# First token steps and first weights loaded by SyncE as fp32, token steps split between SyncE and GpSimd, casts on three engines

## The chip, the cores and the metric

One core of one Trainium2 chip runs the kernel. The metric is the device time of one execution in microseconds (us). The kernel before takes 766.0 us, the median of three runs from 765.8 to 766.04.

The engines are named as in the profile: PE is TensorE's matmuls, PEld its weight loads, DVE is VectorE, ACT is ScalarE, POOL is GpSimd, SP is SyncE.

## The reference

A causal convolution over tokens with seven taps per head (a softmax over the taps), followed by a gated feed-forward layer:

```python
w = softmax(weight)                          # (8 heads, 7 taps)
x_pad = concatenate([zeros((B, 6, D)), x])   # x: (8, 4096, 192)
out[b, s, h, g] = sum_k w[h, k] * x_pad[b, s + k, h, g]   # 24 channels a head
x = out.reshape(32768, 192)
gate = maximum(x @ w_gate, 0)                # w_gate: (192, 1536)
val = x @ w_val                              # w_val:  (192, 1536)
return (gate * val) @ w_out                  # w_out:  (1536, 192)
```

All inputs and the output are fp32. The kernel computes in fp16 with fp32 sums.

## The kernel before

**Tiling.** The eight sequences are two streams of four: stream 0 is batches 0 to 3, stream 1 batches 4 to 7, and both are worked on side by side. 192 channels are three groups (c) of 64; stream 0 sits in partitions 0 to 63, stream 1 in 64 to 127. A unit is 1024 tokens of each stream, in two windows of 512, and there are 16 units. For each window `gate_val` makes the hidden values: for each of twelve slices f of 128 hidden columns, six matmuls with Wg and six with Wv (L541), a ReLU on ScalarE (L552) and a product on VectorE (L553). `project` then multiplies with Wo (L570) and writes the result.

**The weights.** Wg and Wv are held in fp16 twice, in partitions 0 to 63 and 64 to 127, since the two streams need them on their own halves of the array. `load_w(s)` (L167) loads slice s of both, cut at columns 0, 128, 384, 640, 896, 1152 and 1536, by GpSimd with a cast to fp16 on the way, into the lower half. `both_halves` (L175) copies a slice to the upper half: on VectorE for slices 0 and 1, on GpSimd (`pool_halves`) for the others. Slice 0 serves f = 0, slice 1 serves f = 1 and 2, slice 2 serves f = 3 and 4, and so on.

**The convolution.** From the second unit on it is spread over VectorE, ScalarE and GpSimd, with tap values from `tap` (ten small transfers on SyncE, L310, copied to the upper half by GpSimd at L665) and tokens turned by transposing transfers. The first unit has no time for that, so TensorE does it with band matrices: `bands[h]` holds the taps of head h on its diagonals, and x with tokens in partitions is the other operand. A window of 512 tokens is cut in five steps (jj); step 0 has the first 96 tokens of the sequence and no rows ahead of it, steps 1 to 4 have 104 tokens each and 6 rows from before. `conv_dense(0, c, ...)` (L352) does the first window for one c, 40 matmuls in turn over steps and streams; `first_block` (L387) calls it for the three c and copies the result from PSUM to `xc` (L392). The second window (`second_block`) comes between f = 4 and f = 5 of the first.

**The loads at the start.** x of the first window goes to the tile `xts[0]` (`x_h` in the profile; fp16, indices row, step, stream, channel). Stream 0's steps 1 to 4 are loaded by SyncE as fp32 (L122) into `stage`, which is a piece of the tile `room` (`prods` in the profile) that has no other use until later; step 0 of both streams likewise (L138). ScalarE casts the former to fp16 (L317, in two pieces by channels), VectorE the latter (L335). Stream 1's steps 1 to 4 are loaded by GpSimd with the cast on the way (L127). The order is written by hand (`manual_schedule`): every engine executes its instructions in the order in which the program issues them, and an instruction that waits holds all that is behind it on its engine. At the start these orders are:

- SyncE: the taps' weights (L101), stream 0's steps 1 to 4 (L122), step 0 of both streams (L138), the ten `tap` transfers (L310).
- GpSimd: a memset (L126), stream 1's steps 1 to 4 (L127), the select for `spaced` (L128), weight slices 0, 1, 2 (each Wg then Wv), the tokens of the second window (`load_x(1)`, L86), slice 3, the copies of slice 2, slice 4, and so on.
- ScalarE: the softmax' exponentials, the casts of L317, bands of heads 4 to 7 (L329), then copies of `xc`.
- VectorE: the small chain to the band matrices (ending at L329 for heads 0 to 2), the cast of L335, the band of head 3, the copies of slice 0 of Wg and Wv, one `xc` copy, the copies of slice 1.
- TensorE: matmuls without use that keep it busy (L154), the matmuls that make the bands (L272, L292), the 120 convolution matmuls, then L541.

In `conv_dense` the first c takes steps 1 to 4 of stream 0, steps 1 to 4 of stream 1, and step 0 of both; the other c take steps 1, 2, 3, 4, 0 with both streams in each:

```python
late = (1, 2, 3, 4, 0)
both = [(jj, (0, 1)) for jj in late]
if g == 0 and c == 0:
    both = [(jj, (st,)) for st in range(2) for jj in late[0:4]] + both[4:]
```

For f = 0 of the first window the gate and value matmuls go c by c, so that the first needs only the first 64 channels of `xc`, and slice 0 of Wg and Wv in both halves.

## Time and profile before

| what | value |
|---|---|
| median of three runs | 766.0 us |
| span of the profiled execution | 764.4 us |
| TensorE busy | 760.3 us, 99% of the span |
| VectorE, ScalarE, GpSimd busy | 705.6, 600.9, 378.4 us |
| bytes moved by the transfers | 56.00 MB |
| granted TensorE clock in the page's 40 slices | 9 tenths or more in each |

Times in the timeline and in the chain are microseconds from the start of the span: first the start, then the length, then the engine, the line of the kernel, the operation, what it writes and reads, its shape and how many are merged in the line. What stands in brackets is idle time of the engine just before, and what ended it. A line that issues a transfer shows how long the issue took on its engine, not when the data lands; that is in the list of transfers, as the time from issue to landing in the last column. A line of the windows has the stretch, its length, the busy time of the engines with the number of instructions in brackets, the granted clock, the share of the transfer engines and GB/s.

### The profile page before, as it was taken

What the parts mean: (1) busy time and instruction counts of PE and PEld (TensorE: products, weight loads), DVE (VectorE), ACT (ScalarE), POOL (GpSimd) and SP (SyncE); (2) the same over time, 40 slices, a digit from 0 to 9 for tenths busy, and PEclk for the clock granted to TensorE, in tenths of its full rate; (3) what the DMA queues carried; (4) which work ended last, traced back from release to release, by engine and by line L of the source; (5) the groups of instructions that cost most, each with busy time, mean ns of one, the idle gap of its engine ahead of it and who ended that gap; (6) DMA issues with size and microseconds to landing.
All of it is one profiled execution on the core that took longest, in us unless ns stands there. A gap on an engine that the chain in (4) does not pass through costs nothing.

```text
span 764.4 us, 25103 instructions
## 1 busy us (share of the span) xinstructions
PE 760.3 (99%) x10929; PEld 501.3 (66%) x10929; DVE 705.6 (92%) x763; ACT 600.9 (79%) x735; POOL 378.4 (50%) x244
## 2 busy tenths in 40 slices
PE   9999999999999999999999999999999999999998
PEld 5494674947649476584855848567494674947648
DVE  7998999999999999999999999999999999999891
ACT  6787887878878887887878878787787887876571
POOL 9419448093571926729175390853909347090000
PEclk9999999999999999999999999999999999999999
DMA  9969039290452805528073271722819134220202
GB/s 123 134 102 148 7 96 81 65 111 22 95 67 83 97 23 107 49 85 94 30 112 40 85 94 44 120 16 90 89 44 125 13 97 60 66 48 15 71 1 84
DMA packets 131830, 56.00 MB, mean 73 GB/s; under 512 B 96392, under 2 KB 131720, under 8 KB 131720
## 3 DMA queue, kind: packets, MB, share of 16 engines
q1 hardware_dynamic: 90680, 38.81, 23.9%
q0 software_dynamic: 40896, 15.50, 20.3%
q8 instruction: 85, 1.39, 0.8%
q14 instruction: 25, 0.20, 0.1%
q10 hardware_dynamic: 144, 0.10, 0.0%
HBM read 31.48 MB, written 25.17 MB: 74 GB/s over the span
## 4 chain that ended last, share of the span: by engine, by line
PE 99%; DVE 0%; ACT 0%; issue 0%
PE ps L541 65%; PE ps L570 32%; PE ps L619 1%; PE ps L377 0%; PE ps L154 0%; PE ps L411 0%; DVE band L329 0%; PE ps L272 0%; ACT acc L596 0%; PE ps L292 0%
## 5 line engine op out<-in xcount | busy, mean ns | idle before, releaser
L553 DVE TENSOR_TENSOR hT<-gr,ps 128x1024 f16<-128x1024 f16 (+1 forms) x386 | 469.0, 1216 | 36.6 <-ACT gr L552 9.4
L552 ACT ACTIVATE gr<-ps 128x1024 f16<-128x1024 f32 (+1 forms) x386 | 392.9, 1019 | 101.9 <-PE ps L541 99.7
L491 POOL TENSOR_TENSOR prods<-prods 128x1344 f32<-128x1344 f32 x70 | 212.4, 3034 | 290.0 <-DVE prods L487 286.7
L541 PE MATMUL ps<-xc,Wg 64*128 64x512 f16 x2304 | 311.9, 376 | 0.0
L541 PE MATMUL ps<-xc,Wv 64*128 64x512 f16 x2304 | 311.9, 376 | 0.0
L570 PEld LDWEIGHTS <-hT 64*128 64x128 f16 x5952 | 245.9, 94 | 3.7
L570 PE MATMUL ps<-Wo,hT 64*128 64x192 f16 x5952 | 248.1, 243 | 0.0
L541 PEld LDWEIGHTS <-Wv 64*128 64x128 f16 x2304 | 129.8, 94 | 118.5 <-DVE hT L553 0.3
L541 PEld LDWEIGHTS <-Wg 64*128 64x128 f16 x2304 | 112.3, 94 | 132.8 <-issue 0.2
L515 DVE SCALAR_TENSOR_TENSOR acc<-x_r,tap,acc 128x576 f32<-128x576 f16 x225 | 165.3, 813 | 0.0
L485 ACT ACTIVATE prods<-x_r,tap 128x448 f32<-128x448 f16 x222 | 130.1, 660 | 0.0
L596 ACT COPY out_s<-ps 128x768 f32<-128x768 f32 (+1 forms) x64 | 45.5, 711 | 51.3 <-PE ps L570 40.0
L203 POOL DMA_DIRECT2D x_e<-in_x_dram x58 | 47.0, 823 | 16.6 <-ACT acc L501 12.8
L465 POOL COPY x_p<-x_e 128x960 f16<-128x960 f16 (+1 forms) x58 | 50.3, 906 | 1.2 <-DMA x_e<-in_x_dram 1.1
L491 POOL TENSOR_TENSOR xc<-prods 128x1344 f16<-128x1344 f32 x14 | 42.4, 3029 | 1.1
L515 DVE SCALAR_TENSOR_TENSOR xc<-x_r,tap,acc 128x576 f16<-128x576 f16 x45 | 34.1, 813 | 0.0
L501 ACT ACTIVATE acc<-x_r,tap 128x576 f32<-128x576 f16 x45 | 31.4, 763 | 0.0
L487 DVE TENSOR_SCALAR prods<-x_r,tap 128x448 f32<-128x448 f16 x70 | 26.6, 450 | 0.0
L596 DVE COPY out_s<-ps 128x384 f32<-128x384 f32 (+1 forms) x16 | 8.7, 541 | 11.9 <-PE ps L619 9.4
L619 PE MATMUL ps<-Wo,hT 128*128 128x192 f16 x96 | 8.1, 246 | 0.0
L619 PEld LDWEIGHTS <-hT 128*128 128x128 f16 x96 | 7.9, 98 | 0.2 <-issue 0.2
L154 PE MATMUL ps<-const-bfloat16-1.0 128*128 128x512 bf16 (+1 forms) x9 | 3.9, 572 | 0.8 <-PEq L719 0.8
(54 smaller groups left out, 56.3 us busy)
## 6 DMA issues: line engine op xcount, KB each, us to landing
out_dram<-out_s SPq DMA_DIRECT2D x62, 384.0 KB, 2.7
x_e<-in_x_dram POOLq DMA_DIRECT2D x34, 192.0 KB, 7.4
x_e<-in_x_dram POOLq DMA_DIRECT2D x24, 240.0 KB, 5.6
x_r<-x_p SPq DMA_TRANSPOSE x131, 5.1
Wo<-in_moe_w_out_dram POOLq DMA_DIRECT2D x1, 576.0 KB, 7.3
x_h<-in_x_dram POOLq DMA_DIRECT2D x2, 210.0 KB, 4.8
Wg<-in_moe_w_gate_dram POOLq DMA_DIRECT2D x4, 96.0 KB, 4.1
Wv<-in_moe_w_val_dram POOLq DMA_DIRECT2D x4, 96.0 KB, 4.0
```

The costliest lines, as they stand in the source:

```text
L203: first = nc.gpsimd.dma_start(out=xe[:, j0 + start : j0 + n, st, :, :].rearrange("p j c r -> p j (c r)"), in_=bass.AP(tensor=x.tensor, off ...
L465: nc.gpsimd.tensor_copy(out=xp[:, j0 : j0 + n, :, st, :], in_=xe[:, j0 : j0 + n, st, :, :])
L485: engine.activation(out=out, in_=in_, func=ACTF.Copy, scale=scale)
L487: engine.tensor_scalar(out=out, in0=in_, scalar1=scale, scalar2=None, op0=ALU.mult)
L491: nc.gpsimd.tensor_tensor(out=pr[:, 0] if k < KW - 1 else xc[v + 1][:, :, LDVE:UNIT], in0=pr[:, 0], in1=pr[:, k], op=ALU.add,)
L501: nc.scalar.activation(out=accs[v][:, c, :], in_=shifted(v, c, 0, 0), func=ACTF.Copy, scale=tap[:, c, 0:1],)
L515: nc.vector.scalar_tensor_tensor(out=xc[v][:, c, 0:LDVE] if k == KW - 1 else acc[:, c, :], in0=shifted(v, c, k, 0), scalar=tap[:, c, k : k ...
L541: nc.tensor.matmul(out=pss[i][:, st, :], lhsT=W[64 * st : 64 * st + 64, c, 128 * f : 128 * (f + 1)], rhs=xcb[64 * st : 64 * st + 64, c, WI ...
L552: nc.scalar.activation(out=gr[:, sts], in_=pss[0][:, sts], func=ACTF.Relu)
L553: nc.vector.tensor_tensor(out=h[:, f, sts], in0=gr[:, sts], in1=pss[1][:, sts], op=ALU.mult)
L570: mm = nc.tensor.matmul(out=outs[q], lhsT=h[64 * r : 64 * r + 64, f, st, 128 * q : 128 * (q + 1)], rhs=Wo[64 * r : 64 * r + 64, f, :], sta ...
L596: one(out=dst[:, step * j : step * j + step], in_=src[:, step * j : step * j + step])
```

## The change

SyncE loads steps 1 and 2 of stream 0 and, as a transfer of its own, steps 1 and 2 of stream 1, both as fp32 to `stage`. GpSimd loads steps 3 and 4 of stream 0 with the cast on the way, then makes the select, then loads steps 3 and 4 of stream 1.

After step 0 of both streams SyncE loads weight slice 0 of Wg and of Wv as fp32, to places behind `stage` in the same tile (`first_w`). GpSimd's `load_w(0)` and VectorE's copies of slice 0 go away. `cast_w` writes both halves of a slice 0 from `first_w`, two casts each: Wv's on GpSimd, after `load_w(2)` and ahead of `load_x(1)`; Wg's on VectorE, where the copies were.

ScalarE casts steps 1 and 2 of stream 0, the same of stream 1, and step 0 of both, which VectorE did before. The first window's convolution takes the steps in the order 1, 2, 0, 3, 4 with both streams in each, for all three c; the second window's order stays.

```diff
@@ -112,19 +112,20 @@
 
     xts[0] = xpool.tile([128, GSUB, 2, D], F16, name="x_h")
 
-    def body(st):
+    def body(st, jj):
         return bass.AP(
             tensor=x.tensor,
-            offset=x.offset + (NB * st * S + FIRST - PAD) * D,
-            ap=[[D, SUB], [DSUB * D, GSUB - 1], [1, D]],
-        )
-
-    nc.sync.dma_start(out=stage(0, SUB, 0, 1, 1, GSUB - 1), in_=body(0))
+            offset=x.offset + (NB * st * S + FIRST - PAD + DSUB * (jj - 1)) * D,
+            ap=[[D, SUB], [DSUB * D, 2], [1, D]],
+        )
+
+    for st in range(2):
+        nc.sync.dma_start(out=stage(0, SUB, st, 1, 1, 2), in_=body(st, 1))
     ones = const.tile([128, SUB], FP)
     nc.vector.memset(ones[:], 1.0)
     spaced = const.tile([SUB, KW, SEG + 2 * GAP], FP)
     nc.gpsimd.memset(spaced[:], 0.0)
-    nc.gpsimd.dma_start(out=xts[0][0:SUB, 1:GSUB, 1, :], in_=body(1))
+    nc.gpsimd.dma_start(out=xts[0][0:SUB, 3:GSUB, 0, :], in_=body(0, 3))
     nc.gpsimd.affine_select(
         out=spaced[:, :, GAP : GAP + SEG],
         in_=ones[0:SUB, 0 : KW * SEG].rearrange("p (k s) -> p k s", k=KW),
@@ -134,6 +135,7 @@
         base=0,
         channel_multiplier=1,
     )
+    nc.gpsimd.dma_start(out=xts[0][0:SUB, 3:GSUB, 1, :], in_=body(1, 3))
     nc.vector.memset(stage(0, 32, 0, 2, 0, 1), 0.0)
     nc.sync.dma_start(
         out=stage(PAD, FIRST, 0, 2, 0, 1),
@@ -141,6 +143,19 @@
             tensor=x.tensor, offset=x.offset, ap=[[D, FIRST], [NB * S * D, 2], [1, D]]
         ),
     )
+
+    def first_w(i):
+        at = room[0:64, 0, 0, 0:1]
+        return bass.AP(
+            tensor=at.tensor,
+            offset=at.offset + 2 * D * GSUB + NCH * 128 * i,
+            ap=[at.ap[0], [128, NCH], [1, 128]],
+        )
+
+    for i, src in enumerate((moe_w_gate, moe_w_val)):
+        nc.sync.dma_start(
+            out=first_w(i), in_=src.rearrange("(c p) f -> p c f", p=64)[:, :, 0:128]
+        )
     spare = const.tile([H, 1], FP)
     nc.scalar.activation(spare[:], ones[0:H, 0:1], ACTF.Exp)
 
@@ -218,9 +233,13 @@
                     )
                 yield
 
-    load_w(0)
+    def cast_w(copy, i):
+        for p0 in (0, 64):
+            copy(out=(Wg, Wv)[i][p0 : p0 + 64, :, 0:128], in_=first_w(i))
+
     load_w(1)
     load_w(2)
+    cast_w(nc.gpsimd.tensor_copy, 1)
     load_rest(load_x(1))
     load_w(3)
     pool_halves(2)
@@ -313,11 +332,13 @@
             )
             r += n
 
-    for cols in (slice(0, 64), slice(64, D)):
+    for st in range(2):
         nc.scalar.copy(
-            out=xts[0][0:ROWS0, 1:GSUB, 0, cols],
-            in_=stage(0, ROWS0, 0, 1, 1, GSUB - 1)[:, :, cols],
-        )
+            out=xts[0][0:ROWS0, 1:3, st, :], in_=stage(0, ROWS0, st, 1, 1, 2)
+        )
+    nc.scalar.copy(
+        out=xts[0][0 : FIRST + PAD, 0, :, :], in_=stage(0, FIRST + PAD, 0, 2, 0, 1)
+    )
     bands = {}
 
     def fill_band(a, heads, copy):
@@ -332,9 +353,6 @@
         )
 
     fill_band(0, [0, 1, 2], nc.vector.tensor_copy)
-    nc.vector.tensor_copy(
-        out=xts[0][0 : FIRST + PAD, 0, :, :], in_=stage(0, FIRST + PAD, 0, 2, 0, 1)
-    )
     fill_band(0, [3], nc.vector.tensor_copy)
     fill_band(1, [4, 5], nc.scalar.copy)
     fill_band(1, [6, 7], nc.scalar.copy)
@@ -349,26 +367,18 @@
     PLACE = {0: (0, 0, 0), 1: (0, 0, 1), 3: (0, 1, 0), 4: (0, 1, 1)}
     PLACE |= {6: (1, 0, 0), 7: (1, 0, 1), 2: (1, 1, 0), 5: (1, 1, 1)}
 
-    def conv_dense(g, c, ps, bank):
+    def conv_dense(g, c, ps, bank, steps=(1, 2, 3, 4, 0)):
 
 
         xt = xts[g]
-        if g == 0 and c == 0:
-            xc[0] = xcpool.tile([128, NCH, UNIT], F16, name="xc")
-            both_halves(nc.vector.tensor_copy, 0, Wg)
-            both_halves(nc.vector.tensor_copy, 0, Wv)
         toks = GROUPS[g][1]
         t0 = toks[0]
         ends = toks[1:] + [t0 + WIN]
-        late = (1, 2, 3, 4, 0)
-        both = [(jj, (0, 1)) for jj in late]
-        if g == 0 and c == 0:
-            both = [(jj, (st,)) for st in range(2) for jj in late[0:4]] + both[4:]
-        for jj, sts in both:
+        for jj in steps:
             col, n = toks[jj] - t0, ends[jj] - toks[jj]
             rows = n + PAD
             for second in range(2):
-                for st in sts:
+                for st in range(2):
                     for k2 in range(2):
                         k = 2 * c + k2
                         h0, h1 = 32 * k // G, (32 * k + 31) // G
@@ -385,9 +395,11 @@
                         )
 
     def first_block():
+        xc[0] = xcpool.tile([128, NCH, UNIT], F16, name="xc")
+        cast_w(nc.vector.tensor_copy, 0)
         for c in range(NCH):
             ps = psum.tile([128, 2, 512], FP, name="ps")
-            conv_dense(0, c, ps, 0)
+            conv_dense(0, c, ps, 0, (1, 2, 0, 3, 4))
             copy = nc.vector.tensor_copy if c == 1 else nc.scalar.copy
             copy(out=xc[0][:, c, 0:WIN], in_=ps[:, 0, :])
```

## Prediction

> **What bounds the kernel now.** I read the page first, then the chain of waits in order of time, then the timeline of the first 16 us, the same stretch in windows, and the transfers of the first 20 us.

> ```profile
> span 764.4 us, 25103 instructions
> PE 760.3 (99%) x10929; PEld 501.3 (66%) x10929; DVE 705.6 (92%) x763; ACT 600.9 (79%) x735; POOL 378.4 (50%) x244
> ...
> 5.09 0.52 DVE band L329
> ...
> 5.65 2.08 PE ps L377 x106
> 7.72 6.66 PE ps L541 x60
> ...
> 57.46 31.08 PE ps L541 x288
> 88.54 15.84 PE ps L570 x384
> ```

> TensorE is busy for 760.3 of 764.4 us. The last two lines are one unit of the steady part, 31.08 + 15.84 = 46.92 us, and the chain never leaves TensorE there. The edit touches nothing from the second unit on. Its whole effect is the moment at which the first gate and value matmul (L541) starts, 7.66 us, and whether TensorE then runs on.

> ```profile
> 5.12 0.92 ACT L317 CAST x_h<-prods 110x256 f16<-110x256 f32 x2 [1.60 <-DMA prods<-in_x_dram]
> 5.58 0.45 PEld L377 LDWEIGHTS <-x_h 110*32 110x32 f16 x16 [0.42 <-ACT x_h L317]
> 5.67 0.36 DVE L335 CAST x_h<-prods 102x384 f16<-102x384 f32 x1
> 5.95 0.27 DVE L329 CAST band<-ps 128x112 f16<-128x112 f32 x1
> 5.96 0.58 ACT L329 CAST band<-ps 128x224 f16<-128x224 f32 x2
> 6.18 1.38 PEld L377 LDWEIGHTS <-x_h 110*32 110x32 f16 x104 [0.15 <-DMA x_h<-in_x_dram]
> 6.49 0.28 DVE L177 COPY Wg<-Wg 64x384 f16<-64x384 f16 x1 [0.27 <-DMA Wg<-in_moe_w_gate_dram]
> 6.75 0.58 DVE L177 COPY Wv<-Wv 64x384 f16<-64x384 f16 x1
> 7.66 0.39 PE L541 MATMUL ps<-xc,Wg 64*128 64x512 f16 x2
> ...
> 5.65:5.97 0.32, 0.32 (x15) 0.32 (x16) 1.00 1.69 165
> 5.97:6.18 0.21, 0.21 (x10) 0.06 (x4) 1.00 1.55 182
> 6.18:7.66 1.48, 1.48 (x105) 1.38 (x104) 1.00 1.42 174
> ```

> Two things precede 7.66. The band (DVE, 5.09 to 5.61) releases the first convolution matmul at 5.65; its chain comes from the small softmax, and the edit leaves it alone. Then 120 convolution matmuls run (L377). The last three lines are that stretch cut in three windows: 16 weight loads, a gap of 0.21 us in which almost nothing is loaded, then 104 loads in 1.48 us, 14.2 ns each. The gap ends with the arrival of stream 1 from GpSimd. So 0.21 us is all that the convolution waits for data. The 1.48 us are work, so without any wait the start would move from 7.66 to 7.45, no further.

> **The change, the loads first.**

> ```profile
> x_h<-in_x_dram POOLq DMA_DIRECT2D x2, 210.0 KB, 4.8
> ...
> x_h<-in_x_dram POOLq DMA_DIRECT2D x1, 168.0 KB, 4.7
> prods<-in_x_dram SPq DMA_DIRECT2D x1, 144.0 KB, 4.0
> ...
> Wg<-in_moe_w_gate_dram POOLq DMA_DIRECT2D x1, 48.0 KB, 3.8
> Wv<-in_moe_w_val_dram POOLq DMA_DIRECT2D x1, 48.0 KB, 3.4
> ...
> 1.28 0.34 SPq L122 DMA_DIRECT2D prods<-in_x_dram  x1
> 1.42 0.88 POOL L127 DMA_DIRECT2D x_h<-in_x_dram  x1 [0.28 <-issue]
> 1.67 0.48 SPq L138 DMA_DIRECT2D prods<-in_x_dram  x1
> 2.39 0.36 POOL L128 TENSOR_SCALAR_AFFINE_SELECT spaced<-ones 112x112 f32<-112x112 f32 x1
> 2.67 0.68 POOL L170 DMA_DIRECT2D Wg<-in_moe_w_gate_dram  x1
> ...
> 3.55 7.28 SPq L310 DMA_DIRECT2D tap<-taps  x10
> ```

> The last figure of the first rows is the time from issue to landing, so stream 1 lands at 1.42 + 4.7 = 6.12, the first rows at 1.67 + 4.0 = 5.67, the first Wg at 2.67 + 3.8 = 6.47, and Wv, issued 0.67 later, at 3.34 + 3.4 = 6.74.

> SyncE now issues five transfers ahead of the taps where it had two. At 0.34 to 0.48 each the three more take about 1.1 us, so the last issue ends near 3.3, before the taps are due at 3.55; these cost nothing. Both streams' steps 1 and 2 have together the rows of the old single transfer, so I let the second land when that did: ScalarE's first cast waited for it until 5.12. The first rows are as many rows into the queue as before: 5.67. Steps 3 and 4 of stream 1 are now behind a second GpSimd issue, after the select, at about 2.5 instead of 1.42, and share the engines with 96 KB of half-precision weights that are now 192 KB of fp32 on SyncE's queue. Their landing, which I call L, is the price that the trace does not show. From below it is 6.12, since the bytes of x ahead of it are the same; from above 6.74, by when the old kernel had landed all of x and the same weights.

> ```profile
> q0 software_dynamic: 319, 0.12, 100.9%
> q1 hardware_dynamic: 140, 0.09, 40.7%
> ```

> These are the queues from 4.1 to 5.1 us: GpSimd's (q0) and SyncE's (q1) move packets at the same time, so the weights take their share before GpSimd's last steps are through. I take L = 6.5, nearer to the upper row, because all the bytes that landed by 6.74 are asked for before those steps can finish.

> [...]

> **The casts.**

> ```profile
> L317 ACT CAST x_h<-prods x2: 405/508/612, 5.1 to 5.4; 110x256 f16<-110x256 f32 x1, 110x512 f16<-110x512 f32 x1
> ```

> ScalarE has three casts of 384 elements in place of 256 and 512. Between 405 and 612 ns that is 0.51 us each. Stream 0 arrives earlier and is cast while ScalarE was idle; stream 1 from 5.12 to 5.63, in time for TensorE at 5.65 but for some 0.04; the first rows, once VectorE's work in 0.36 (L335), from 5.67 to 6.18. Bands 4 to 7 follow, 0.58 us, until 6.76 instead of 6.54; they are needed by the second and third 64 channels, after 6.7, so this is covered.

> TensorE now takes steps 1 and 2 of both streams (16 matmuls, 5.65 to 5.97), waits for the first rows until 6.18 + 0.05 = 6.23 (the 0.05 is the distance from ScalarE's first cast, ended at 5.53, to the load at 5.58), does those 8, and waits for L. After L come 16 + 80 = 96 matmuls, 96 x 14.2 ns = 1.37 us. The gate starts at 6.5 + 0.04 + 1.37 = 7.91, where it was 7.66: **+0.25 us**. At L = 6.12 the first rows bind instead: 6.23 + 104 x 14.2 ns = 7.71, +0.05. At L = 6.74 it is 8.15, +0.49. The new order of steps costs nothing itself: the same 120 matmuls.

> **First weights and the GpSimd queue.**

> ```profile
> 5.82 0.63 POOL L170 DMA_DIRECT2D Wv<-in_moe_w_val_dram  x1
> 6.44 1.63 POOL L86 DMA_DIRECT2D x_h<-in_x_dram  x2
> 10.14 0.82 POOL L177 COPY Wv<-Wv 64x768 f16<-64x768 f16 x1
> ...
> 12.27 0.81 PE L541 MATMUL ps<-xc,Wv 64*128 64x512 f16 x6
> 14.31 1.55 PE L377 MATMUL ps<-band,x_h 110*32 110x104 f16 x120
> ...
> 23.03 0.25 POOL L665 COPY tap<-tap 64x21 f32<-64x21 f32 x1
> ```

> VectorE casts Wg twice; at the 0.36 of L335 that is 0.72 us after a landing near 6.5, done by 7.2, before 7.91. GpSimd casts Wv twice. Its issues end earlier than before, at 1.42 + 0.66 + 0.45 + 0.66 + 4 x 0.63 = 5.71 (0.66 for a half load, between 0.63 and 0.88), but the cast waits for Wv, near 6.6. For 384 elements, half of the 768 in 0.82, I take 0.41 (from above 0.82, since the input is twice as wide). Both are done at 7.42, 0.5 before TensorE wants them: nothing. From above: 6.74 + 1.64 = 8.38, and 8.43 against 7.91 costs 0.52 more.

> Behind these casts on GpSimd stand the loads of the second 512 tokens, which start at 7.42 instead of 6.44, and all later weights, 0.98 late. The Wv copy at 10.14 ends at 10.96 and is read at 12.27: 1.31 us of cover. The second load of tokens, issued near 7.25, lands 4.8 later at 12.05 and is read at 14.31: 2.26. The taps land by about 15 and are copied at 23.03. All stay covered; were the cover gone, each later microsecond would stop TensorE for one.

> **The sum.** 764.4 + 0.25 = 764.65 for the profiled span. The runs' median of 766.0 lies 1.6 above the span, so **766.25**.

> **The rivals.**
> *The convolution gains.* Both waits shrink: transfers by SyncE land a few tenths earlier and L falls under 6.0. At most the whole gap goes: 7.45, or 765.8. For it: two of five steps no longer need the late GpSimd transfer. Against: the first rows must then be cast before 5.97, and they land at 5.67.
> *The casts on GpSimd are late.* With the price from above the gate starts at 8.43, +0.77, or 766.8. For it: the copy of Wv on VectorE took 0.58 where the equal one of Wg took 0.28, while GpSimd was busy; so work on the two can hold each other up. If the two VectorE casts go first, GpSimd ends at 7.42 + 0.72 = 8.14, +0.53, or 766.5. [...]
> *The weights starve.*

> ```profile
> Wv<-in_moe_w_val_dram POOLq DMA_DIRECT2D x2, 96.0 KB, 3.3
> ```

> If SyncE's weights are served only behind all that GpSimd has queued, Wv lands with the old transfer of 5.82, at 9.1. With 0.82 for casts the gate starts at 9.97, +2.3, or 768.3: clearly **slower**. It decides from a landing near 8.4, where 1.5 us are lost. Against: q1 did move 0.09 MB beside q0.
> *Nothing happens* is the near end of the forecast (+0.05).

> **How the numbers follow.** Forecast (+0.05 to +0.5) 0.5; convolution gains 0.22; GpSimd casts late 0.2; weights starve 0.06; something outside this list 0.02. A measurement of this kernel can tell some 0.2% from no change, which is 1.53 us. The gain is bounded by 0.21 plus what little the first unit loses later, so faster gets 0.02. Slower needs the starving weights or a GpSimd queue that eats its whole cover: 0.07. Same gets 0.91. The likeliest case's own range is 766.0 to 766.5. For 8 in 10 I reach below to 765.5 (the gap gone, and the spread of the runs) and above to 767.1 (late casts, and half of what lies beyond).

> **What would show it.** Right: the chain is TensorE's again; the convolution's weight loads show two short waits, for ScalarE near 6.2 and for x_h near 6.5; the first L541 near 7.9; steady units of 46.92. Wrong: a first L541 before 7.6 or after 8.4, a wait of L541 for GpSimd's cast, a gap at 11.6 to 14.3, or any unit that isn't 46.92.

## The result and the profile after

The changed kernel takes 769.48 us (median of five runs, 768.7 to 771.09) against 766.0 for the kernel before (five runs, 765.69 to 766.15). The ratio is 1.0049, with a 95% interval of 1.0037 to 1.0062: slower by about 3.5 us, and outside the predicted range of 765.5 to 767.1.

The profiled execution took 770.42 us, 0.9 above the median of its kernel. Its page begins with the span and the busy times:

```profile
span 768.3 us, 25105 instructions
PE 763.5 (99%) x10929; PEld 502.6 (65%) x10929; DVE 705.5 (92%) x762; ACT 602.1 (78%) x736; POOL 378.5 (49%) x245
```

The span is 3.9 us longer and TensorE is busy 3.2 us longer, with the same 10929 matmuls. So much of the loss is not idle time: the same work took longer. The chain of waits of the changed kernel says where (start, length, what; the convolution is now L387, gate and value L553, the output L582):

```profile
2.64 4.81 DMA x_h<-in_x_dram
7.45 0.04 issue
7.50 2.24 PE ps L387 x65
9.73 8.32 PE ps L553 x60
18.05 1.48 PE ps L387 x120
...
61.11 31.08 PE ps L553 x288
92.19 15.84 PE ps L582 x384
```

The steady unit is still 31.08 + 15.84 = 46.92 us. The second window's convolution (120 matmuls, 1.48 us, also unchanged) starts at 18.05 where it started at 7.72 + 6.66 = 14.38. These 3.67 us are nearly the whole loss: of the 3.9 us by which the span is longer, all but 0.2 arise in the first 18 us. (The chain ends with a copy on ScalarE, from 761.40 before and from 765.05 now; what the span has beyond that comes after it.) Two things are new there. The chain now begins with a transfer, the last steps of stream 1. And the 60 gate and value matmuls behind it take 8.32 us, where 60 of them took 6.66 before.

The timeline of the changed kernel from 2.6 to 10 us shows what was late:

```profile
2.64 0.70 POOL L138 DMA_DIRECT2D x_h<-in_x_dram  x1
2.65 0.77 SPq L156 DMA_DIRECT2D prods<-in_moe_w_gate_dram  x1
...
3.47 0.62 SPq L156 DMA_DIRECT2D prods<-in_moe_w_val_dram  x1
...
5.79 0.51 ACT L339 CAST x_h<-prods 102x384 f16<-102x384 f32 x1 [0.77 <-DMA prods<-in_x_dram]
...
6.35 0.21 PEld L387 LDWEIGHTS <-x_h 102*32 102x32 f16 x10 [0.15 <-ACT x_h L339]
7.49 2.00 PEld L387 LDWEIGHTS <-x_h 110*32 110x32 f16 x94 [0.93 <-DMA x_h<-in_x_dram]
7.50 2.24 PE L387 MATMUL ps<-band,x_h 110*32 110x104 f16 x94 [0.71 <-DMA x_h<-in_x_dram]
7.67 1.12 DVE L238 CAST Wg<-prods 64x384 f16<-64x384 f32 x2 [1.78 <-DMA prods<-in_moe_w_gate_dram]
...
8.88 1.06 POOL L238 CAST Wv<-prods 64x384 f16<-64x384 f32 x2 [3.06 <-DMA prods<-in_moe_w_val_dram]
...
9.66 0.61 PE L553 MATMUL ps<-xc,Wg 64*128 64x512 f16 x2
```

Stream 1's last steps, issued at 2.64, landed at 7.45; the prediction had 6.5. TensorE waited 0.93 us for them. Wg was there at 7.67 and Wv at 8.88, and each of their casts took over half a microsecond (1.12 and 1.06 for two). The first two L553 came at 9.66 instead of 7.66, and take 0.61 where the same two took 0.39. That TensorE ran at half speed, and until when, is seen best in two windows of equal length (start and end, length, busy time of TensorE's matmuls, of its weight loads, of VectorE, ScalarE and GpSimd, each with the number of instructions, the granted clock, the transfers' share and GB/s):

```profile
9.82:13.23 3.41, 3.41 (x18) 1.30 (x17) 1.30 (x3) 1.63 (x3) 3.41 (x6) 1.00 0.55 58
13.24:16.65 3.41, 3.41 (x36) 1.49 (x32) 2.71 (x5) 2.61 (x4) 3.41 (x6) 1.00 1.34 159
```

TensorE is busy throughout in both, with 18 gate and value matmuls in the first and 36 in the second.

### The profile page after: what moved, and what is told of

It reads as the page before. It is cut to its first block, busy times and chain, and to the rows that moved or that the text cites. A ratio compares the mean times of both kernels' runs of the same rounds, so it can differ in the third digit from the quotient of the medians.

```text
span 768.3 us, 25105 instructions
## 1 busy us (share of the span) xinstructions
PE 763.5 (99%) x10929; PEld 502.6 (65%) x10929; DVE 705.5 (92%) x762; ACT 602.1 (78%) x736; POOL 378.5 (49%) x245
## 4 chain that ended last, share of the span: by engine, by line
PE 99%; DMA 1%; issue 0%; POOL 0%; ACT 0%; POOLq 0%
PE ps L553 65%; PE ps L582 32%; PE ps L631 1%; DMA x_h<-in_x_dram 1%; PE ps L387 0%; PE ps L423 0%; POOL spaced L127 0%; ACT acc L608 0%; POOL spaced L129 0%; POOLq L129 0%; POOL x_h L128 0%; POOLq L731 0%
## 5 line engine op out<-in xcount | busy, mean ns | idle before, releaser
L553 PE MATMUL ps<-xc,Wg 64*128 64x512 f16 x2304 | 313.0, 377 | 0.0
L553 PE MATMUL ps<-xc,Wv 64*128 64x512 f16 x2304 | 312.5, 377 | 0.0
L582 PEld LDWEIGHTS <-hT 64*128 64x128 f16 x5952 | 245.9, 94 | 3.7
L582 PE MATMUL ps<-Wo,hT 64*128 64x192 f16 x5952 | 248.1, 243 | 0.0
L553 PEld LDWEIGHTS <-Wv 64*128 64x128 f16 x2304 | 130.1, 94 | 119.4 <-issue 1.0
L553 PEld LDWEIGHTS <-Wg 64*128 64x128 f16 x2304 | 112.1, 94 | 133.3 <-issue 1.1
L218 POOL DMA_DIRECT2D x_e<-in_x_dram x58 | 46.6, 816 | 16.5 <-ACT acc L513 13.2
L387 PE MATMUL ps<-band,x_h 110*32 110x104 f16 (+7 forms) x240 | 4.7, 247 | 0.7 <-DMA x_h<-in_x_dram 0.7
```

Source lines behind the costliest of these rows:

```text
L218: first = nc.gpsimd.dma_start(out=xe[:, j0 + start : j0 + n, st, :, :].rearrange("p j c r -> p j (c r)"), in_=bass.AP(tensor=x.tensor, off ...
L553: nc.tensor.matmul(out=pss[i][:, st, :], lhsT=W[64 * st : 64 * st + 64, c, 128 * f : 128 * (f + 1)], rhs=xcb[64 * st : 64 * st + 64, c, WI ...
L582: mm = nc.tensor.matmul(out=outs[q], lhsT=h[64 * r : 64 * r + 64, f, st, 128 * q : 128 * (q + 1)], rhs=Wo[64 * r : 64 * r + 64, f, :], sta ...
```

## The experiments

Four explanations could each carry some of the loss. Theory A: the bytes that SyncE now fetches hold up stream 1's last steps. Theory B: those steps are late because their issue moved behind the select, from 1.42 to 2.64. Then, the weights: they land late and are cast one after the other. And theory C, the clock: a longer wait of TensorE brings its clock down, so that a wait costs more than itself. The expectations call the first gate and value matmul L541, its line in the kernel before; in the timelines it has the line of each run's own kernel. The kernel before, run along with each group of experiments, had medians of 765.96, 766.07 and 766.07 us (21, 17 and 14 runs). All kernels compute the whole reference. Each profile shows one execution, so an event can lie some tenths of a us elsewhere in the next one.

**The kernel before again (e0_before).** No edit.

> The kernel before, unchanged, for a second profile of its clock. If the moment at which TensorE's matmuls turn to full speed is set by the kernel's own work, 512-column matmuls are at 0.38 us from about 4.8 us again, the first L541 starts near 7.66 and the span is near 764.4. If it is a matter of chance, the moment lies elsewhere and the span is longer by a microsecond or more in some profiles.

It took 765.96 us, with a span of 764.2, and full speed came between 4.18 and 5.04, as in the first profile (119 convolution matmuls then took 1.90 us). But the convolution had no wait for stream 1 this time, and the gate started at 7.42 instead of 7.66:

```profile
7.42 0.39 PE L541 MATMUL ps<-xc,Wg 64*128 64x512 f16 x2
```

Half of this lead was lost again: the second window's convolution started at 14.25 instead of 14.38. So the same program's gate start varies by 0.24 from one execution to the next. Of the 21 runs beside it 19 lie between 765.73 and 766.2, and two at 767.78 and 767.87: now and then the kernel before, too, loses almost 2 us.

**Slice 0 of the weights back on GpSimd, everything else as changed (e1_w_gpsimd, and g1_w_gpsimd once more).**

```diff
-    for i, src in enumerate((moe_w_gate, moe_w_val)):
-        nc.sync.dma_start(out=first_w(i), in_=...)
+    load_w(0)
     load_w(1)
     load_w(2)
-    cast_w(nc.gpsimd.tensor_copy, 1)
...
-        cast_w(nc.vector.tensor_copy, 0)
+        both_halves(nc.vector.tensor_copy, 0, Wg)
+        both_halves(nc.vector.tensor_copy, 0, Wv)
```

> The changed kernel, but slice 0 of the weights is loaded by GpSimd with the cast on the way and copied by VectorE, as before. Theory A (SyncE's weight transfers beside GpSimd's slow both queues): the last steps of stream 1 land by 6.3 us in place of 7.45, the first L541 starts at 7.6 to 7.9, span within 0.5 us of before's, time 766.0 to 766.6. Theory B (stream 1's last steps are late because they are issued behind the select, at 2.64): they land after 7 again and the time stays at 768.5 or above.

> The changed kernel with slice 0 of the weights by GpSimd again, for a second profile: its first one had full speed only at 10.0 us. If full speed comes at 4 to 5 us here, stream 1's last steps land near 6.2, TensorE waits less than 0.4 us in the convolution, the first L541 starts near 7.9 and the span is near 764.8.

e1 took 766.77 us (766.48 to 768.28, eleven runs; ratio 1.0014, 1.0005 to 1.0023), g1 766.68: most of the loss is gone, a little stays (the time expected by theory A was 766.0 to 766.6). The timeline of g1:

```profile
2.64 0.70 POOL L138 DMA_DIRECT2D x_h<-in_x_dram  x1
...
6.18 1.42 PE L383 MATMUL ps<-band,x_h 102*32 102x96 f16 x104 [0.30 <-ACT x_h L335]
...
7.54 0.39 PE L550 MATMUL ps<-xc,Wg 64*128 64x512 f16 x2
...
8.43 0.51 DVE L188 COPY Wg<-Wg 64x768 f16<-64x768 f16 x1 [0.52 <-DMA Wg<-in_moe_w_gate_dram]
```

Stream 1's last steps were issued at 2.64 as in the changed kernel, but now the convolution waits only for ScalarE's cast of the first rows and then runs through. So the later issue (theory B) alone is not what delays them: they landed 3.7 us after it, and 4.8 after it in the changed kernel. The first gate matmul comes at 7.54, between the 7.66 and the 7.42 of the two profiles of the kernel before, and the second window's convolution at 14.37, like theirs (14.38 and 14.25). So neither a gain nor a loss by splitting x and by the new order of steps shows in the first unit. The second GpSimd issue for x puts off every weight behind it, and slice 1 of Wg is copied only from 8.43; but where the 0.6 to 0.8 us that stay in the time come from, these profiles do not settle. In e1's profile TensorE was at half speed until 10.0 us, without a long wait, and there the 120 convolution matmuls took 2.96 us:

```profile
5.89 2.96 PE L383 MATMUL ps<-band,x_h 110*32 110x104 f16 x120
```

**The fp32 weights alone (e2_w_sync_x_old).** The kernel before with the changed kernel's weights; x as before.

```diff
+    for i, src in enumerate((moe_w_gate, moe_w_val)):
+        nc.sync.dma_start(out=first_w(i), in_=...)
...
-    load_w(0)
     load_w(1)
     load_w(2)
+    cast_w(nc.gpsimd.tensor_copy, 1)
...
-            both_halves(nc.vector.tensor_copy, 0, Wg)
-            both_halves(nc.vector.tensor_copy, 0, Wv)
+            cast_w(nc.vector.tensor_copy, 0)
```

> The kernel before, but slice 0 of the weights comes by SyncE as fp32 behind step 0, with the casts of the changed kernel (Wg on VectorE, Wv on GpSimd). x, its casts and the order of steps are as before. Theory A: the second stream's four steps land at 6.8 or later in place of 6.12, TensorE waits for them, time 767.5 to 770. Theory B: they land at 6.1 to 6.3 and the time is 766.0 to 766.6.

It took 767.91 us (767.37 to 769.77, eleven runs; ratio 1.0025, 1.0016 to 1.0034). The landing that theory A expected here failed to come late: stream 1, issued at 1.41 ahead of SyncE's weights, was there at 6.09, as in the kernel before, and the convolution was on time. That the time lies within theory A's range is therefore luck. Together with g1 it says that it took both: SyncE's weights did not delay stream 1 when it was issued at 1.41, and the issue at 2.64 did no harm without them (landing near 6.3). (Here stream 1 is also one load and not a second half; no run separates that.) The time went elsewhere, as its timeline shows:

```profile
6.98 1.12 DVE L235 CAST Wg<-prods 64x384 f16<-64x384 f32 x2 [1.05 <-DMA prods<-in_moe_w_gate_dram]
7.58 0.39 PE L556 MATMUL ps<-xc,Wg 64*128 64x512 f16 x1
...
7.98 1.06 POOL L235 CAST Wv<-prods 64x384 f16<-64x384 f32 x2 [2.77 <-DMA prods<-in_moe_w_val_dram]
...
9.09 0.09 PEld L556 LDWEIGHTS <-Wv 64*128 64x128 f16 x1 [0.47 <-POOL Wv L235]
```

Its chain of waits ends on the same thing:

```profile
2.99 4.93 DMA prods<-in_moe_w_val_dram
...
9.09 6.58 PE ps L556 x57
15.67 1.48 PE ps L392 x116
```

The first gate matmul is on time at 7.58, and then the gate waits for Wg's second cast and for both of Wv's until 9.09. The second window's convolution starts at 15.67, 1.29 later than in the kernel before, which is most of the 1.6 us by which this profile's span is longer. In the median the weights cost 767.91 - 765.96 = 1.95 us by themselves, with x on time.

**TensorE kept at work during the wait (e3_fill).** The changed kernel with three matmuls that nothing reads ahead of step 3 of the first c.

```diff
         for jj in steps:
+            if g == 0 and c == 0 and jj == 3:
+                warm_up(512, 512, 512)
```

> The changed kernel, with three 512-column matmuls without use put ahead of steps 3 and 4 of the first 64 channels, where TensorE waits for stream 1. Theory C (a good part of the loss is TensorE's clock, held low after that wait): the wait is filled, full speed comes by about 9.8 instead of 13.2, and the time falls by 1 to 2 us against the changed kernel, to 767 to 768.5. Rival (the loss is the wait alone): the time stays within 0.5 us of the changed kernel's or grows by up to 0.7.

It took 768.58 us (768.23 to 768.86, five runs; ratio 1.0033, 1.0021 to 1.0046): 0.9 less than the changed kernel, though it does more, and its five runs lie within 0.63 us where those of the changed kernel spread over 2.4. The expected fall was 1 to 2 us, and the intervals of the two ratios overlap, so the clock's share is made likely here, not measured. Timeline of e3:

```profile
6.96 1.28 PE L389 MATMUL ps<-band,x_h 110*32 110x104 f16 x96
...
8.69 1.06 POOL L238 CAST Wv<-prods 64x384 f16<-64x384 f32 x2 [2.87 <-DMA prods<-in_moe_w_val_dram]
...
9.24 0.09 PEld L555 LDWEIGHTS <-Wv 64*128 64x128 f16 x1 [0.85 <-POOL Wv L238]
...
9.80 0.09 PEld L555 LDWEIGHTS <-Wv 64*128 64x128 f16 x1 [0.47 <-POOL Wv L238]
```

96 convolution matmuls take 1.28 us, full speed, but now the gate stands at 9.24 and 9.80 for GpSimd's casts of Wv. The two delays of the changed kernel lie over each other: with the clock held, the late weights decide. In this execution stream 1's last steps landed 4.2 us after their issue at 2.65, at 6.85, although the transfers are those of the changed kernel.

**One GpSimd transfer for x and three on SyncE (f2_one_gpsimd_x).** A try for something better than both: the kernel before with its weights left on GpSimd, and x's steps 3 and 4 of stream 0 also on SyncE. (Beside these lines, ScalarE casts three pieces, one for each SyncE transfer, and the first c takes the steps 1, 2, 3, 4, 0 with both streams in each, as the others do.)

```diff
-    nc.sync.dma_start(out=stage(0, SUB, 0, 1, 1, GSUB - 1), in_=body(0))
+    for st, jj in ((0, 1), (1, 1), (0, 3)):
+        nc.sync.dma_start(out=stage(0, SUB, st, 1, jj, 2), in_=body(st, jj))
...
-    nc.gpsimd.dma_start(out=xts[0][0:SUB, 1:GSUB, 1, :], in_=body(1))
+    nc.gpsimd.dma_start(out=xts[0][0:SUB, 3:GSUB, 1, :], in_=body(1, 3))
```

> The kernel before, with x split otherwise: SyncE loads steps 1 and 2 of both streams and steps 3 and 4 of stream 0, GpSimd one transfer with steps 3 and 4 of stream 1; the weights stay with GpSimd, whose queue issues as many transfers as before. If what harms in the changed kernel's x is the extra GpSimd issue (0.7 us for half the rows, and all weights behind it later by as much), this one has the gain without the cost: the last steps land by 5.9, the convolution runs without a wait, first L541 near 7.5, time 765.7 to 765.9. If SyncE's larger share of x is itself the harm, the time is 766.3 or more.

It took 768.66 us (766.98 to 770.84, six runs; ratio 1.0039, 1.0025 to 1.0053). The hoped-for gain failed; the time is that of the other branch, 766.3 or more. In its timeline the extra bytes on SyncE's queue hold up that queue itself, first stream 0's last steps, then the first rows (in the kernel before ScalarE's casts of stream 0 began at 5.12, VectorE's of the first rows at 5.67):

```profile
6.08 0.51 ACT L318 CAST x_h<-prods 110x384 f16<-110x384 f32 x1 [1.06 <-DMA prods<-in_x_dram]
6.41 0.36 DVE L335 CAST x_h<-prods 102x384 f16<-102x384 f32 x1 [0.71 <-DMA prods<-in_x_dram]
...
6.64 1.51 PE L375 MATMUL ps<-band,x_h 110*32 110x104 f16 x104 [0.26 <-ACT x_h L318]
```

This profile is of the fastest of the six runs (766.98), with its first gate matmul at 8.08. What the other five lost beyond it, 0.6 to 3.9 us, it cannot show.

**A cold start (f3_cold).** The kernel before without the first seven matmuls, which nothing reads.

```diff
-    warm_up(512, 512, 512, 512, 512, 512, 256)
```

> The kernel before without its first seven matmuls without use, so that TensorE has little to do until 3.7 us; transfers and casts are as before. Theory C (clock): full speed comes only after a long busy stretch, at 9 us or later, with the first L541s 0.4 us apart a pair in place of 0.2; time 767.5 to 769, about where before's own two slow executions lie (767.8). Rival (the clock costs little at this point): 766.0 to 766.6.

It took 766.85 us (766.48 to 767.55, ten runs; ratio 1.0009, 1.0001 to 1.0018). Its timeline has the 120 matmuls of the convolution in 3.08 us; from the first of them to the first gate matmul the kernel before needed 7.66 - 5.65 = 2.01, its wait of 0.21 included:

```profile
5.77 3.08 PE L376 MATMUL ps<-band,x_h 110*32 110x104 f16 x120
```

So half speed that ended soon after the convolution (at 9.4 us in this profile) cost 0.8 us of the median, less than theory C expected and more than its rival did. In the changed kernel's first profile it lasted into the gate, until 13.2, and there 60 gate and value matmuls took 8.32 us instead of 6.66.

**The weights without slices 1 and 2 beside them (f4_w_alone).** The changed kernel with `load_w(1)` and `load_w(2)` behind the casts of Wv on GpSimd.

```diff
+    cast_w(nc.gpsimd.tensor_copy, 1)
     load_w(1)
     load_w(2)
-    cast_w(nc.gpsimd.tensor_copy, 1)
```

> The changed kernel, with GpSimd's loads of weight slices 1 and 2 put behind its casts of Wv, so that SyncE's weights have only x beside them. If SyncE's weights land late because they share the engines with GpSimd's slices 1 and 2, Wv lands by 7.0 in place of 8.82 and the first GpSimd cast begins then. If they are slow by themselves, Wv lands after 8 again. The time says little here, since slices 1 and 2 come later than TensorE wants them: over 769.

It took 769.58 us in its one run; much of the loss is a new one, since the gate now waits for slice 1 (until 11.12, 1.01 us at the last). The lines to read are these of its timeline:

```profile
7.00 1.27 PE L387 MATMUL ps<-band,x_h 110*32 110x104 f16 x94 [0.42 <-DMA x_h<-in_x_dram]
...
7.38 1.06 POOL L238 CAST Wv<-prods 64x384 f16<-64x384 f32 x2 [4.04 <-DMA prods<-in_moe_w_val_dram]
...
8.21 0.53 PE L553 MATMUL ps<-xc,Wg 64*128 64x512 f16 x2
```

Wv's cast starts at 7.38 instead of 8.88, later than the 7.0 expected, but early enough to say that slices 1 and 2, which GpSimd fetches at the same time, delay Wv by 1.0 (against f5, below) to 1.5 us. x came at 7.00, against 7.26 and 7.49 in the changed kernel's two profiles but 6.85 in e3, which also has the slices beside it; so no part of x's delay is shown to be theirs. The 94 convolution matmuls at full speed are also the measure for the changed kernel: 1.27 here, 2.24 there.

**The changed kernel again (f5_after).** No edit.

> The changed kernel again, for a second profile. If the late full speed of the first profile (13.2 us) is a matter of where the clock's interval falls, it may come at 4 to 5 us here; then the first L541 starts near 8.2, TensorE waits for GpSimd's cast of Wv until 9.5 or later, and the span is near 766.9. If it belongs to the kernel, it is at 13 us again, span near 768.3.

768.73 us, span 767.0. The span is near the expected 766.9, but not for the expected reason: the first gate matmul came at 9.43, not near 8.2, and no wait for Wv followed. In this profile the clock changes in plain view. Its windows, with the columns as above:

```profile
3.85:7.27 3.42, 2.07 (x48) 1.29 (x48) 1.21 (x4) 1.91 (x5) 1.96 (x4) 1.00 1.12 173
7.27:10.68 3.41, 3.41 (x100) 2.48 (x102) 2.89 (x5) 1.17 (x2) 2.20 (x4) 0.50 0.67 90
10.68:10.75 0.07, 0.07 (x4) 0.06 (x2) 0.00 (x0) 0.00 (x0) 0.07 (x1) 1.00 0.00 0
```

In the first stretch TensorE had full speed (one 512-column matmul took 0.39 us at 4.05) and was busy for 2.07 of 3.42 us, since it waited for x_h from 6.3 to 7.26 (0.93 in its timeline). In the next 3.41 us it was busy without a break, and had half speed (granted clock 0.50). Then full speed came back. So the wait of 0.93 us cost itself, and then half of the 3.41 us behind it: an estimated 1.7 us, since at half speed that stretch does the work of 1.7.

**SyncE's weight transfers beside kernel e1, read by nobody (g2_w_beside).**

```diff
+    for i, src in enumerate((moe_w_gate, moe_w_val)):
+        nc.sync.dma_start(out=first_w(i), in_=...)
```

> That kernel (slice 0 by GpSimd, cast on the way) with SyncE's two fp32 weight transfers put back behind step 0, though nothing reads them: only their traffic is added, no cast and no wait. Theory A (the traffic delays stream 1's last steps, 6.24 without it, 7.2 to 7.45 in the changed kernel): they land at 6.9 or later, TensorE waits 0.6 us or more, time 767.5 to 769.5, in place of 766.8. Rival (the loss of the changed kernel is all in the late casts of the weights): the steps land by 6.4, time 766.5 to 767.2.

It took 769.54 us (768.68 to 770.2, four runs; ratio 1.0045, 1.0031 to 1.0058): as great a loss as the changed kernel's, by traffic alone, with no cast of e1 changed. It carries slice 0 twice, by SyncE and by GpSimd, so it has more traffic than the changed kernel. Its timeline, to be held against that of g1:

```profile
6.86 0.51 ACT L339 CAST x_h<-prods 102x384 f16<-102x384 f32 x1 [1.78 <-DMA prods<-in_x_dram]
...
7.42 2.40 PE L387 MATMUL ps<-band,x_h 102*32 102x96 f16 x104 [0.98 <-ACT x_h L339]
```

And the queues from 4.5 to 7.0 us (packets, MB, time of the packets as a share of 16 engines), first of g1, then of g2:

```profile
q0 software_dynamic: 806, 0.26, 108.2%
q1 hardware_dynamic: 158, 0.06, 10.5%
```

```profile
q0 software_dynamic: 574, 0.18, 79.3%
q1 hardware_dynamic: 474, 0.23, 38.6%
```

GpSimd's queue (q0) moved 0.26 MB in these 2.5 us without SyncE's weights and 0.18 with them, while SyncE's (q1) went from 0.06 to 0.23. In the changed kernel they moved 0.17 and 0.18. Stream 1's last steps landed 4.7 us after their issue at 2.66, near 7.4, against 3.7 after 2.64 in g1, near 6.3: theory A's landing. (The median of GpSimd's two loads of x, from issue to landing, is 4.1 in g2 and 3.7 in g1.) But the wait that counted here was another one: the first rows, ahead of the weights on SyncE's own queue, were cast only at 6.86 (5.62 in g1, 5.79 in the changed kernel), and the convolution took them up at 7.42, when the last steps had landed.

**As many bytes, but rows of x (g3_x_beside).** Like g2, with transfers of 768-byte rows in place of the weights.

```diff
+    for i in range(2):
+        nc.sync.dma_start(out=..., in_=...)   # 64 x 2 rows of x, behind first window
```

> As the kernel beside it, but the added traffic is as many bytes of x in rows of 768 B (256 packets in place of 384 of 512 B), into the same place and read by nothing. If any bytes on SyncE's queue delay GpSimd's, stream 1's last steps land at 6.9 or later and the time is within 0.5 us of that kernel's. If it is the number of packets or the weights' short rows, they land at 6.3 to 6.7 and the time is nearer to 766.8.

It took 767.9 us (767.8 to 771.74, seven runs; ratio 1.0035, 1.0023 to 1.0048). The last steps of stream 1 land 4.7 us after their issue, as with the weights, so for them the size and kind of the pieces made no difference; with no added bytes beside them (g1) it was 3.7. The time lies 1.6 us below that of g2, not within 0.5; here the first rows were on time (cast at 5.57), and the clock held. Its timeline and its windows:

```profile
7.43 1.31 PE L397 MATMUL ps<-band,x_h 110*32 110x104 f16 x94 [0.99 <-DMA x_h<-in_x_dram]
```

```profile
5.46:8.87 3.41, 2.42 (x125) 1.68 (x123) 1.01 (x4) 1.68 (x5) 3.41 (x6) 1.00 1.35 181
```

Here TensorE waited as long (0.99) and kept full speed: 94 matmuls in 1.31 us. In the stretch of 3.41 us around the wait it was busy for 2.42 us. So a wait of 0.99 us left the clock alone in this profile. The first gate matmul then came at 8.67, 1.01 later than in the kernel before; then the gate stood 0.33 us, until 9.62, for an `xc` copy on VectorE, which came behind the copy of Wv, also held up (8.56 instead of 6.88 in g1).

**Only x late (g4_x_late).** The kernel before with GpSimd's load of stream 1 behind its loads of slice 0; no traffic added, no cast changed.

```diff
-    nc.gpsimd.dma_start(out=xts[0][0:SUB, 1:GSUB, 1, :], in_=body(1))
...
     load_w(0)
+    nc.gpsimd.dma_start(out=xts[0][0:SUB, 1:GSUB, 1, :], in_=body(1))
```

> The kernel before, with GpSimd's load of stream 1 put behind its loads of slice 0; all else as before, so SyncE loads no weights and no cast changes. The steps land near 6.9 and TensorE waits for them about 0.9 us in the place where it waits 0.2. If the wait alone counts, the time is 766.5 to 767.0 in all runs. If such a wait also costs the clock (theory C), some executions show half speed for an interval of 3.4 us behind it and lie 1 to 2 us higher: median 767 to 768.5, spread over 1 us.

It took 768.27 us (767.48 to 770.39, seven runs; ratio 1.003, 1.0018 to 1.0042). The timeline, then the windows:

```profile
7.30 2.65 PE L377 MATMUL ps<-band,x_h 110*32 110x104 f16 x104 [1.20 <-DMA x_h<-in_x_dram]
```

```profile
4.03:7.44 3.41, 1.97 (x40) 1.28 (x41) 1.87 (x7) 1.42 (x4) 3.41 (x6) 1.00 1.23 141
7.44:10.86 3.42, 3.42 (x110) 2.71 (x108) 1.69 (x3) 1.17 (x2) 2.85 (x5) 0.50 1.40 160
```

Again full speed, a stretch with TensorE busy for 1.97 of 3.41 us, and half speed in the next. The last steps landed later than expected (near 7.3 instead of 6.9). Nothing but the wait, 1.20 us here, was added, and every one of the seven runs lies above the 767.0 that the wait alone allowed, also with 0.3 more for its greater length: so the wait cost the clock by itself here.

## Why the prediction was wrong

*The bound.* Right: only the start of the first gate matmul and the first unit behind it matter, steady units stay at 46.92, and the second window's convolution follows the first's f = 4 without a gap. The start came at 9.66, beyond the 8.4 that the prediction named as showing it wrong.

*The landing L.* This is the first step that failed: "I take L = 6.5", with 6.74 as the upper bound, "by when the old kernel had landed all of x and the same weights". It was 7.45, in f5 about 7.2 and in e3 6.85, always above that bound. The row of 6.74 bounds nothing, because in the old kernel the weights stood behind stream 1 on one queue, and were half as many bytes as the profile counts them (48 KB and 96 KB a piece). Here the bytes on the other queue were served beside x, not behind it: g2 puts back those bytes alone, and from 4.5 to 7.0 us GpSimd's queue moved 0.18 MB instead of 0.26 while SyncE's moved 0.23 instead of 0.06; the last steps landed near 7.4 instead of 6.3. The lower bound, "since the bytes of x ahead of it are the same", was near what happens without these bytes (6.3 in g1). The late issue has its part: in e2, with the same bytes beside it, the whole of stream 1, issued at 1.41, was there at 6.09.

*A wait costs its own length.* This step was never written down as one: the sum took a microsecond of waiting for x as a microsecond, and the clock did not occur in it. With the 94 matmuls of f4 (7.00 to the first gate matmul at 8.21) the profiled 3.67 us split like this. From 7.49 the gate would have started at 7.49 + 1.21 = 8.70 at full speed, 1.04 later than before: the late landing. It started at 9.66, 0.96 more: the convolution at half speed. The 60 matmuls behind it took 8.32 instead of 6.66, 1.66 more: the gate at half speed, with a wait of 0.20 for Wv within. These are 3.66 together, and some 2.4 to 2.6 of them are the clock. Not all of that belongs to the wait: e1, which has no long wait, also did its convolution at half speed (2.96 us for the 120 matmuls). In the changed kernel's first profile full speed came only at 13.2 us, in f5 it was there by 4.05 and until 7.27. The two are the same program, whose stretches ended at other moments (13.23 and 7.27, for instance), so how much of the clock a run loses is in part chance. The profile that is split here is of a run 0.9 us above the median.

*The weights.* "Wv, near 6.6" failed: the cast began at 8.88 (8.42 in f5, 7.98 in e2). The issues on SyncE, 0.77 and 0.62 instead of 0.34 to 0.48, moved the taps from 3.55 to 4.13, which cost nothing. Casts of 384 elements were put at 0.36 on VectorE and 0.41 on GpSimd; they took 0.56 and 0.53. The rival of starving weights, at 768.3 and a chance of 0.06, came near the times of e2 (767.91) and e3 (768.58), though not by its mechanism, service only behind all that GpSimd had queued: both queues moved packets at the same time. Its point of decision, a landing at 8.4, was passed in the changed kernel and in e3 (casts from 8.69); in e2 7.98 was enough, as the two casts take 1.06 rather than 0.82. In the changed kernel this loss lies under the other one: with x on time (e2) 1.95 us stay, with the clock held (e3) 2.6, and with the weights back on GpSimd (e1) 0.8.

*The casts and the queue of GpSimd.* Right: ScalarE's 0.51 for 384 elements, the first rows' cast near its place (5.79 to 6.30, step 0 at 6.35), the second load of tokens later on GpSimd (issued at 9.88 instead of 6.44, more than the 0.98 foreseen) and still in time for 18.05. Too low: 0.66 for the issue of half a load; 0.86 and 0.70, as against 0.88 for a whole one. So the split in two nearly doubled what this load cost on GpSimd, 1.56 against 0.88. In g1 TensorE's weight loads then wait 0.20 us for each copy of slice 1, but the second window starts no later for it. The pair of 0.28 and 0.58 us, read as VectorE and GpSimd holding each other up, was 0.28 and 0.28 in e0, with the same GpSimd issue beside it; so the one pair does not show it.

*The convolution gains.* This rival did not show. In the changed kernel the wait grew; without SyncE's weights (g1) the start of 7.54 lies within what the kernel before does by itself (7.42 to 7.66). The 0.21 us that it hoped to win were gone in e0 anyway, and that run took 765.96, no less than the median.

## What to carry to other kernels

Before a load is moved to an idle queue, count the bytes that then compete with the transfer on the critical path: here SyncE's weights moved the landing of stream 1's last steps from near 6.3 (g1) to near 7.4 (g2). A landing read from a trace holds only for the traffic of that trace, and here it varied by up to 0.6 us between executions of the same transfers (7.45 in the changed kernel's first profile, 6.85 in e3). A wait of TensorE near the start has to be priced with the clock: here waits of 0.93 us (f5) and 1.20 us (g4) were followed by 3.41 and 3.42 us at half speed, an estimated 1.7 us more, and one of 0.99 us (g3) was not. Three matmuls that nothing reads, put into the wait, seem to have taken that part away in e3, where the 96 convolution matmuls behind it took 1.28 us. And a difference of 0.1 or 0.2 us between two profiles says nothing before the kernel before has been profiled twice.

## What the runs showed of the hardware

```profile
2.99:6.40 3.41, 3.41 (x41) 1.82 (x43) 1.94 (x7) 1.94 (x5) 2.83 (x5) 1.00 1.01 186
```

It counts as busy throughout, and yet the convolution behind it ran at half speed. What decides stays open. The granted clock of the page reads 1.00 in the changed kernel's first profile although 18 matmuls took as long there as 36 did later; such counts, or the durations of single matmuls, tell the speed.

That the two queues together moved less in the changed kernel than in the kernel before (0.17 + 0.18 = 0.35 MB from 4.5 to 7.0 us, against 0.43 + 0.02 = 0.45) was not expected either. SyncE's weights are not the reason, since g1 moved 0.26 + 0.06 = 0.32 without them. What is stays open: the sizes of the pieces differ between the kernels, and no run separates that.

No version tried beats the kernel before. The nearest one that moves loads is e1, 0.8 us behind it.
